# Attention and two feed-forward layers on one core: weights decoded in pairs of chunks, through two raw buffers of 1 MB

## The chip, the core and the metric

One core of a Trainium2 chip runs the whole program. The metric is the device time of one execution in microseconds. A kernel's time is the median over its runs, and one further execution is taken with the hardware profiler; all rows shown come from that one.

## The reference

Inputs are float32. Attention has no softmax over scores: q is normalised by exp over its feature axis, k by exp over the sequence, and the product is q (k^T v). Two feed-forward layers follow on all 2304 tokens.

```python
q_s = exp(q - max(q, -1)); q_s /= sum(q_s, -1) + 1e-9      # (4, 8, 576, 64)
k_s = exp(k - max(k, 2));  k_s /= sum(k_s, 2) + 1e-9
x = q_s @ (k_s^T @ v)                                      # to (2304, 512)
h = x @ w_in1;  x = (h * sigmoid(1.702 h)) @ w_out1        # w_in (512, 2048)
h = x @ w_in2;  out = (h * tanh(softplus(h))) @ w_out2     # w_out (2048, 512)
```

The four weight matrices reach the kernel as float64, so it must decode them on the chip. It makes two float32r parts of each weight, a high one and the rest, and forms each product from three matmuls (high x high, high x rest, rest x high; `SPLIT`).

## The kernel before

Tokens are cut into 6 blocks of 384 (`NB`), the feed-forward width into 16 chunks of 128 (`NFC`). For each block, `attention(blk)` makes the block's x in the buffer `xt[blk % 2]`. The first layer then runs over block and chunk: `gemm_in1(n)` (L755, 12 matmuls of 384 columns), `gelu` and `gelu_split` (L768, L773 and the lines of `copy` and `either`), and `gemm_out` (L796, 12 matmuls) two chunks later. All these GEMMs write the key `spine`, so they keep their order on TensorE. `x2_evac` stores the layer's result. The second layer does the same by pairs of chunks (`gemm_in2`, `mish`, `gemm_out2` at L927) and `out_evac` copies the result through the tiles `dec` to the output.

**Weights.** `weight(m, io, fc)` (L366) decodes one chunk of w_in (`io` 0) or w_out (`io` 1), 512 weights per partition. A DMA on SP's queue (L320) brings 512 KB into one of four buffers `raw`; each weight is two 32-bit words, `lo_w` and `hi_w`, which lie alternately. Then come:

- two scalings, normally on ScalarE (L346): `hi_w` into one of three tiles `dec`, `lo_w` in place in `raw`;
- on VectorE the fast shift (L386), the OR with the sign (L393, reads `hi_w`) and the addition of the low word (L398, the last reader of `raw`);
- the copy of the high part into the weight tile `W` (L337, ScalarE or VectorE) and the subtraction that gives the rest (L329, VectorE or GpSimd). This frees `dec`.

Each chunk has one tile `W[fc]` for both its matrices. The first 13 are there from the start; the last three (`NLATE`) use memory that `attention(0)` sets free. The second layer's chunks are decoded into the same tiles as soon as the first layer's last block has read them. `w_order(lag)` gives the order: w_in runs ahead of w_out by 2 chunks in the first layer and 6 in the second.

**Order of the work.** Nothing is issued as the loops reach it. Each operation goes into a `Plan` with its ways (an engine and a cost for each), the keys that it reads and those that it writes. `Plan.order` then plays all engines and the one DMA queue forward by these costs (`act_ns`, `dve_ns`, `pool_ns`, `mm_ns`; a DMA of n bytes counts n / 280 ns and 650 at least), takes the most urgent operation that is ready, and picks the engine where it ends first. `best` does so six times, with urgencies from a pass backwards, and keeps the shortest. `emit` issues the result in that order, so each engine and SP's queue works through a fixed list, and an instruction that waits holds those behind it on its own list. Before the first GEMM the plan also places idle transposes on TensorE (L962).

The buffers are keys like all others; this is what makes a load wait for the addition of the chunk that had its buffer before:

```python
r, a = raw[i % NRAW], dec[i % ND]
rl, rh, da = ("raw", i % NRAW, 0), ("raw", i % NRAW, 1), ("dec", i % ND)
...
dma(P * 4096, [], [rl, rh], lambda: dst, lambda: src)
```

Of the kernel before, what the change touches and what calls it, by code (L numbers as in the profile page):

```python
# [19 lines left out]
class Plan:  # L20
# [13 lines left out]
    def __init__(self):  # L34
        self.ops = []
        self.first = None
        self.last_write = {}
        self.readers = {}
# [37 lines left out]
    def order(self, links, urgency, ways=None):  # L76
# [125 lines left out]
def pool_ns(n):  # L202
    return {512: 1256.0, 384: 972.0, 768: 1800.0}[n]
# [7 lines left out]
def tile_attention_moe_moe(  # L211
# [35 lines left out]
    NLATE = 3  # L247
    NRAW = 4
    WHOLE = 2
    ND = 3  # L250
# [8 lines left out]
    W = [const.tile([P, 2, 1024], F32R, name=f"W{i}") for i in range(NFC - NLATE)]  # L259
# [3 lines left out]
    raw = [const.tile([P, 1024], I32, name=f"raw{i}") for i in range(NRAW)]  # L263
    dec = [const.tile([P, 512], I32, name=f"dec{i}") for i in range(ND)]
# [78 lines left out]
    def scaled(out, in_, scale, reads, writes):  # L343
        plan.op(
            [
                (ACT, act_ns(512), lambda: nc.scalar.activation(out=out, in_=in_, func=AF.Copy, scale=scale), False),  # L346
                (
                    DVE,
                    dve_ns(512, True),
                    lambda: nc.vector.tensor_single_scalar(out=out, in_=in_, scalar=scale, op=ALU.mult),  # L350
                    True,
                ),
            ],
            reads,
            writes,
        )
# [9 lines left out]
    def weight(m, io, fc):  # L366
# [22 lines left out]
        dve(  # L389
            512,  # L390
            [rh],
            [da],
            lambda: nc.vector.scalar_tensor_tensor(  # L393
                out=a, in0=hi_w, scalar=-0x80000000, in1=a, op0=ALU.bitwise_and, op1=ALU.bitwise_or
            ),
            pair=True,
        )
        dve(512, [rl], [da], lambda: nc.vector.tensor_tensor(out=a, in0=a, in1=lo_w, op=ALU.add), pair=True)  # L398
        late = [("late",)] if fc >= NFC - NLATE else []
        copy(512, lambda: W[fc][:, io, 0:512], lambda: f32(a), [da] + late, [("W", io, fc, 0)])  # L400
        either(
            512,
            ALU.subtract,
            lambda: W[fc][:, io, 512:1024],
            lambda: f32(a),
            lambda: f32(W[fc][:, io, 0:512]),
            [da, ("W", io, fc, 0)],
            [("W", io, fc, 1)],
        )

    def w_mm(fc, io, part, c, n=P):
        return W[fc][:, io, part * 512 + c * P : part * 512 + c * P + n]

# [336 lines left out]
    def gemm_in(h, hkeys, buf, fc, ccs=range(NCC)):  # L750
        for cc in ccs:
# [11 lines left out]
            pe(3 * mm_ns(NB), x_keys(buf, cc) + [("W", 0, fc, 0), ("W", 0, fc, 1)], [spine] + hkeys, mm)  # L763
# [26 lines left out]
    def gemm_out(n):  # L790
        fc = n % NFC
        for dm in range(NCC):

            def mm(dm=dm):
# [11 lines left out]
                [("W", 1, fc, 0), ("W", 1, fc, 1), ("g", n % 2, 0), ("g", n % 2, 1)],  # L806
# [32 lines left out]
    ob = [f32(t) for t in dec]  # L839
# [5 lines left out]
    def pool_first():  # L845
        sctx.close()
        late = ctx.enter_context(tc.tile_pool(name="late", bufs=1, side="right", reuse_waits="tile"))
        W.extend(late.tile([P, 2, 1024], F32R, name=f"W{i}") for i in range(NFC - NLATE, NFC))
# [69 lines left out]
    def gemm_out2(n):  # L918
        bi, pr = divmod(n, NPR)
        gi = (n + 1) % NGP  # L920
        for j in range(2):
            for c in range(NCT):
# [12 lines left out]
                wk = [("W", 1, 2 * pr + j, a) for a in range(2)]  # L935
                pe(3 * mm_ns(512), wk + [("gg", gi, 0), ("gg", gi, 1)], [spine, ("acc", bank)], mm)

    def out_evac(bi):
        blk = blocks[bi]
        dst = out[blk * NB : (blk + 1) * NB, :].rearrange("(p c) e -> p c e", c=NCT)  # L940
        for c in range(NCT):
# [8 lines left out]
                [("dec", c)],  # L950
            )
            dma(P * 2048, [("dec", c)], [], lambda c=c: dst[:, c, :], lambda o=o: o)


    def w_order(lag):
        seq = [(0, fc) for fc in range(lag)]
        for fc in range(lag, NFC):
            seq += [(0, fc), (1, fc - lag)]
        return seq + [(1, fc) for fc in range(NFC - lag, NFC)]
# [5 lines left out]
    FIRST_W = 24  # L965
# [10 lines left out]
    for io, fc in w_order(2):  # L976
        weight(0, io, fc)
    second = w_order(6)
# [43 lines left out]
    for n in range(NSB + LAG):  # L1022
        if n < NSB:
            weights_to(FIRST_W + 4 * n)
# [43 lines left out]
```

## Time and profile before

| | before |
|---|---|
| median of 3 runs | 892.43 us |
| lowest, highest | 891.02, 893.08 us |
| profiled execution | 891.93 us, its span 890.2 us |
| busy: PE, DVE, ACT, POOL | 99%, 44%, 41%, 1% of the span |
| raw loads, 512 KB each | 32 of w_in, 32 of w_out; 4.3 and 4.0 us to landing (median) |
| HBM read, written | 54.00 MB, 11.01 MB |

PE stands for TensorE's matmuls, PEld for its weight loads, DVE for VectorE, ACT for ScalarE, POOL for GpSimd, SP for the queue from which all DMAs are issued. The span runs from the first to the last instruction of the program; the execution's own time has a little around it. Busy shares of the whole span mix stages with different limits, so tables by stretch and the chain of waits are read beside them. In the chain, each piece is what the next one waited for, or the instruction before it on the same engine, and its time is what it adds to the chain. The granted clock of TensorE is shown as 1.00 throughout.

### The profile page before, as it was taken

Reading aid. Unit: us, or ns where it says so; the run is one execution under the profiler, and the core shown is the slowest. Engines: PE = TensorE matmul, PEld = TensorE weight load, DVE = VectorE, ACT = ScalarE, POOL = GpSimd, SP = SyncE. Lnnn points to the kernel's source line nnn. Section 1 sums busy time; section 2 is a strip of 40 time slices with the busy share of each in tenths; the row PEclk is TensorE's granted clock in tenths of the full one; section 3 lists DMA queues with packets and bytes.
Section 4 is the critical chain, followed back from the end, with each engine's and each line's share of the span. In section 5 each row is a group of like instructions: output and inputs, shape, how many; then the busy total and the mean of one; then the engine's idle time right before and its main releaser. Section 6 shows DMA issues by size and latency. Waiting matters only on the chain.

```text
span 890.2 us, 12245 instructions
## 1 busy us (share of the span) xinstructions
PE 880.3 (99%) x4961; PEld 818.9 (92%) x4961; DVE 394.6 (44%) x757; ACT 362.7 (41%) x649; POOL 5.3 (1%) x21
## 2 busy tenths in 40 slices
PE   8999999999999999999999999999999999999998
PEld 5897899999999999999999999899899899899896
DVE  7999993263385276226999911101101101111110
ACT  6987863242343244224778821321321321321321
POOL 1000000000000000000000000000000000000000
PEclk9999999999999999999999999999999999999999
DMA  9676762011132022100355301001001001000000
GB/s 259 201 221 175 202 209 70 5 48 55 27 94 95 1 71 55 48 1 18 119 168 187 119 1 71 36 1 71 36 1 71 36 1 71 36 1 0 36 1 36
DMA packets 62712, 65.80 MB, mean 74 GB/s; under 512 B 32448, under 2 KB 53696, under 8 KB 62144
## 3 DMA queue, kind: packets, MB, share of 16 engines
q1 hardware_dynamic: 62656, 65.02, 23.7%
q8 instruction: 39, 0.64, 0.3%
q14 instruction: 17, 0.14, 0.0%
HBM read 54.00 MB, written 11.01 MB: 73 GB/s over the span
## 4 chain that ended last, share of the span: by engine, by line
PE 88%; DVE 7%; ACT 2%; DMA 1%; issue 1%; DVEq 0%; SPq 0%
PE hp L755 23%; PE acc L927 22%; PE acc L796 19%; PE h L755 19%; DVE dec L393 1%; DVE dec L398 1%; PE at L533 1%; DVE W L329 1%; DMA raw<-in_moe_w_in_dram 1%; PE at L667 1%; PE at L638 1%; PE acc L494 1%; DVE gt L773 1%; PE acc L497 1%; DVE dec L386 1%
## 5 line engine op out<-in xcount | busy, mean ns | idle before, releaser
L755 PE MATMUL h<-xt,W 128*128 128x384 f32 x1152 | 224.3, 339 | 1.0 <-DVE gt L773 0.8
L796 PE MATMUL acc<-g,W 128*128 128x384 f32 x1152 | 223.0, 339 | 0.2 <-DVE W L329 0.2
L755 PE MATMUL hp<-xt,W 128*128 128x384 f32 x1152 | 208.4, 335 | 0.0
L927 PE MATMUL acc<-W,g 128*128 128x512 f32 x864 | 206.1, 392 | 0.0
L755 PEld LDWEIGHTS hp<-xt,W 128*128 128x128 f32 x1152 | 201.9, 188 | 3.7
L755 PEld LDWEIGHTS h<-xt,W 128*128 128x128 f32 x1152 | 200.4, 188 | 5.2 <-DVE gt L773 1.1
L796 PEld LDWEIGHTS acc<-g,W 128*128 128x128 f32 x1152 | 200.5, 188 | 2.7 <-issue 0.8
L927 PEld LDWEIGHTS acc<-W,g 128*128 128x128 f32 x864 | 161.6, 188 | 32.7
L329 DVE TENSOR_TENSOR g<-gt,g 128x384 fp32r<-128x384 f32 (+1 forms) x110 | 67.4, 613 | 179.0 <-ACT g L337 178.7
L329 DVE TENSOR_TENSOR g<-tb,g 128x768 fp32r<-128x768 f32 x32 | 30.7, 958 | 211.6 <-ACT g L337 211.6
L904 ACT ACTIVATE tb<-hp 128x768 f32<-128x768 f32 x32 | 26.0, 812 | 177.7 <-PE hp L755 177.7
L337 ACT ACTIVATE g<-gt 128x384 fp32r<-128x384 f32 (+1 forms) x112 | 63.8, 570 | 80.0 <-PE acc L796 77.4
L768 ACT ACTIVATE gt<-h 128x384 f32<-128x384 f32 x96 | 46.9, 488 | 92.7 <-PE h L755 92.6
L773 DVE SCALAR_TENSOR_TENSOR gt<-gt,h 128x384 f32<-128x384 f32 x96 | 52.8, 550 | 63.8 <-ACT gt L768 63.5
L904 ACT ACTIVATE gt<-hp 128x768 f32<-128x768 f32 x16 | 13.0, 814 | 96.3 <-PE hp L755 96.3
L346 ACT ACTIVATE dec<-raw 128x512 f32<-128x512 f32 x64 | 42.9, 675 | 10.1 <-DVE W L329 8.9
L346 ACT ACTIVATE raw<-raw 128x512 int32<-128x512 uint32 x63 | 42.0, 676 | 4.8 <-DMA raw<-in_moe_w_out_dram 3.0
L329 DVE TENSOR_TENSOR W<-dec,W 128x512 fp32r<-128x512 f32 x64 | 43.6, 683 | 0.8 <-ACT W L337 0.5
L398 DVE CUSTOM_DVE_ANT_0 dec<-raw,dec 128x1024 uint16<-128x1024 uint16 x64 | 43.6, 683 | 0.4
L393 DVE SCALAR_TENSOR_TENSOR dec<-raw,dec 128x512 int32<-128x512 int32 x64 | 43.6, 683 | 0.2
L337 ACT ACTIVATE W<-dec 128x512 fp32r<-128x512 f32 x62 | 38.9, 630 | 7.3 <-DVE dec L398 7.3
L337 ACT ACTIVATE g<-tb 128x768 fp32r<-128x768 f32 x32 | 27.1, 847 | 1.0
(78 smaller groups left out, 396.8 us busy)
## 6 DMA issues: line engine op xcount, KB each, us to landing
raw<-in_moe_w_in_dram SPq DMA_DIRECT2D x32, 512.0 KB, 4.3
raw<-in_moe_w_out_dram SPq DMA_DIRECT2D x32, 512.0 KB, 4.0
x2d<-xt SPq DMA_DIRECT2D x16, 384.0 KB, 3.1
xt<-x2d SPq DMA_DIRECT2D x4, 1536.0 KB, 6.5
kt<-in_k_dram SPq DMA_DIRECT2D x16, 288.0 KB, 4.3
out_dram<-dec SPq DMA_DIRECT2D x18, 256.0 KB, 2.1
vt<-in_v_dram SPq DMA_DIRECT2D x24, 144.0 KB, 3.5
qt<-in_q_dram SPq DMA_DIRECT2D x24, 96.0 KB, 2.6
```

Source lines behind the costliest of these rows:

```text
L329: return lambda: engine.tensor_tensor(out=out(), in0=in0(), in1=in1(), op=op)
L337: (ACT, act_ns(n), lambda: nc.scalar.activation(out=out(), in_=in_(), func=AF.Copy), False),
L346: (ACT, act_ns(512), lambda: nc.scalar.activation(out=out, in_=in_, func=AF.Copy, scale=scale), False),
L386: lambda: nc.vector.tensor_single_scalar(out=a, in_=a, scalar=3, op=ALU.logical_shift_left),
L393: lambda: nc.vector.scalar_tensor_tensor(out=a, in0=hi_w, scalar=-0x80000000, in1=a, op0=ALU.bitwise_and, op1=ALU.bitwise_or),
L398: dve(512, [rl], [da], lambda: nc.vector.tensor_tensor(out=a, in0=a, in1=lo_w, op=ALU.add), pair=True)
L755: nc.tensor.matmul(out=h(), lhsT=w_mm(fc, 0, a, cc), rhs=xt[buf][:, cc, b, :], start=cc == 0 and i == 0, stop=cc == NCC - 1 and i == 2,)
L768: act(NB, [hk, ("tables",)], [tk], lambda: nc.scalar.activation(out=t, in_=h, func=AF.Tanh, scale=0.851), psum=True)
L773: lambda: nc.vector.scalar_tensor_tensor(out=t, in0=t, scalar=1.0, in1=h, op0=ALU.add, op1=ALU.mult),
L796: nc.tensor.matmul(out=acc[dm][:, 0:NB], lhsT=w_mm(fc, 1, a, dm), rhs=g[n % 2][:, b, :], start=fc == 0 and i == 0, stop=fc == NFC - 1 and ...
L904: nc.scalar.activation(out=tb[i], in_=hb(n), func=AF.Mish)
L927: nc.tensor.matmul(out=acc[bank], lhsT=g2[gi][:, j, a, c * P : (c + 1) * P], rhs=w_mm(2 * pr + j, 1, b, 0, 512), start=pr == 0 and j == 0 ...
```

## The change

Two neighbouring chunks are decoded together. `weight(m, io, fp)` works on pair `fp` (8 of them, `NFP`): one DMA of 1 MB into one of two buffers `raw` of twice the size, and operations of 1024 elements through two tiles `dec` of twice the size. The DMA of w_in now reads 512 32-bit words of a row where it read 256. `W` becomes a tile per pair and matrix, `W[fp][io]`, with the two chunks side by side; the last two pairs (four chunks) are those that wait for `attention(0)`'s memory. `either` and the scalings are costed for 1024 elements, and POOL has a cost for that length. Waits of matmuls on weights go by pairs (`fc // 2`, `pr`). The lags become 1 and 3 pairs, `FIRST_W` 12 pairs, and `weights_to` grows by 2 pairs per step. A new table `soonest` keeps the first two raw loads from being planned before 12 us. The output goes through halves of the two `dec` tiles, under keys `ob` of its own.

```diff
-    return {512: 1256.0, 384: 972.0, 768: 1800.0}[n]
+    return {1024: 2400.0, 512: 1256.0, 384: 972.0, 768: 1800.0}[n]
...
-                t = 0.0
+                t = 0.0 if ways else self.soonest.get(i, 0.0)
...
-    NLATE = 3
-    NRAW = 4
+    NLATE = 2
+    NRAW = 2
     WHOLE = 2
-    ND = 3
+    ND = 2
+    NFP = NFC // 2
+    FIRST_LOAD = 12000.0
...
-    W = [const.tile([P, 2, 1024], F32R, name=f"W{i}") for i in range(NFC - NLATE)]
+    W = [[const.tile([P, 2, 1024], F32R, name=f"W{i}_{io}") for io in range(2)] for i in range(NFP - NLATE)]
...
-    raw = [const.tile([P, 1024], I32, name=f"raw{i}") for i in range(NRAW)]
-    dec = [const.tile([P, 512], I32, name=f"dec{i}") for i in range(ND)]
+    raw = [const.tile([P, 2048], I32, name=f"raw{i}") for i in range(NRAW)]
+    dec = [const.tile([P, 1024], I32, name=f"dec{i}") for i in range(ND)]
...
         if io == 0:
             dst = r.rearrange("p (cc f) -> p cc f", cc=NCC)
-            src = w_ap[m][0][:, fc * 256 : (fc + 1) * 256].rearrange("(cc p) f -> p cc f", p=P)
+            src = w_ap[m][0][:, fp * 512 : (fp + 1) * 512].rearrange("(cc p) f -> p cc f", p=P)
+            at_w = lambda part: W[fp][0][:, :, part * 512 : (part + 1) * 512].rearrange("p l (cc f) -> p l cc f", cc=NCC)
+            of = f32(a).rearrange("p (cc l f) -> p l cc f", cc=NCC, l=2)
         else:
-            dst = r
-            src = w_ap[m][1][fc * P : (fc + 1) * P, :]
-        dma(P * 4096, [], [rl, rh], lambda: dst, lambda: src)
+            dst = r.rearrange("p (l e) -> p l e", l=2)
+            src = w_ap[m][1][fp * 256 : (fp + 1) * 256, :].rearrange("(l p) e -> p l e", p=P)
+            at_w = lambda part: W[fp][1][:, :, part * 512 : (part + 1) * 512]
+            of = f32(a).rearrange("p (l e) -> p l e", l=2)
+        if i < NRAW:
+            plan.soonest[len(plan.ops)] = FIRST_LOAD
+        dma(P * 8192, [], [rl, rh], lambda: dst, lambda: src)
         scaled(f32(a), f32(hi_w), 2.0**-112, [rh], [da])
         scaled(lo_w, lo_w.bitcast(U32), 2.0**-29, [], [rl])
         dve(
-            512,
+            1024,
...
-        copy(512, lambda: W[fc][:, io, 0:512], lambda: f32(a), [da] + late, [("W", io, fc, 0)])
+        copy(1024, lambda: at_w(0), lambda: of, [da] + late, [("W", io, fp, 0)])
...
-    ob = [f32(t) for t in dec]
+    ob = [f32(dec[c // 2])[:, c % 2 * 512 : (c % 2 + 1) * 512] for c in range(NCT)]
...
-                [("dec", c)],
-            )
-            dma(P * 2048, [("dec", c)], [], lambda c=c: dst[:, c, :], lambda o=o: o)
+                [("ob", c)] + ([("dec", i) for i in range(ND)] if bi == 0 else []),
+            )
+            dma(P * 2048, [("ob", c)], [], lambda c=c: dst[:, c, :], lambda o=o: o)
...
-    FIRST_W = 24
+    FIRST_W = 12
...
-    for io, fc in w_order(2):
-        weight(0, io, fc)
-    second = w_order(6)
+    for io, fp in w_order(1):
+        weight(0, io, fp)
+    second = w_order(3)
...
-            weights_to(FIRST_W + 4 * n)
+            weights_to(FIRST_W + 2 * n)
```

## Rows read from the trace of the kernel before

**Rows 1.** The head of the page: busy us (share of the span) and instructions.

```profile
PE 880.3 (99%) x4961; PEld 818.9 (92%) x4961; DVE 394.6 (44%) x757; ACT 362.7 (41%) x649; POOL 5.3 (1%) x21
```

**Rows 2.** Table by stretches: busy us of PE, PEld, DVE, ACT, POOL; clock; DMA.

```profile
60.00:119.30 59.30, 57.09 (x356) 47.44 (x354) 58.74 (x127) 48.33 (x100) 2.37 (x2) 1.00 0.68 196
119.30:416.00 296.70, 296.70 (x1851) 292.02 (x1852) 148.77 (x305) 109.08 (x220) 0.00 (x0) 1.00 0.18 53
416.00:510.00 94.00, 94.00 (x533) 92.86 (x532) 88.47 (x165) 71.98 (x133) 0.00 (x0) 1.00 0.44 140
```

**Rows 3.** The chain of waits, 34 to 125 us: start us, us, piece.

```profile
37.12 0.47 DVE g L329
37.59 0.60 DVE dec L393
...
40.32 0.60 DVE W L329
...
59.25 4.79 DMA raw<-in_moe_w_in_dram
...
70.94 0.87 DVE qt L329
...
72.42 0.34 DVE dec L386
...
118.61 0.31 ACT kv L556
...
119.89 2.08 PE h L755 x12
```

**Rows 4.** The page's groups: out<-in, shape, count; busy us, mean ns; idle before.

```profile
L329 DVE TENSOR_TENSOR g<-tb,g 128x768 fp32r<-128x768 f32 x32 | 30.7, 958 | 211.6 <-ACT g L337 211.6
...
L346 ACT ACTIVATE dec<-raw 128x512 f32<-128x512 f32 x64 | 42.9, 675 | 10.1 <-DVE W L329 8.9
...
L329 DVE TENSOR_TENSOR W<-dec,W 128x512 fp32r<-128x512 f32 x64 | 43.6, 683 | 0.8 <-ACT W L337 0.5
```

**Rows 5.** DMA issues from 0 to 13 us: count, KB each, median us to landing.

```profile
raw<-in_moe_w_out_dram SPq DMA_DIRECT2D x1, 512.0 KB, 10.8
```

**Rows 6.** Timeline, 9 to 18 us: start us, us, instruction.

```profile
9.53 1.71 SPq L320 DMA_DIRECT2D raw<-in_moe_w_out_dram  x1
...
14.40 0.68 ACT L346 ACTIVATE dec<-raw 128x512 f32<-128x512 f32 x1
```

**Rows 7.** Timeline at the end of the decode, 116 to 128 us.

```profile
118.45 0.68 DVE L398 CUSTOM_DVE_ANT_0 dec<-raw,dec 128x1024 uint16<-128x1024 uint16 x1
...
121.03 0.68 DVE L329 TENSOR_TENSOR W<-dec,W 128x512 fp32r<-128x512 f32 x1
...
121.81 2.25 PE L796 MATMUL acc<-g,W 128*128 128x384 f32 x12
```

**Rows 8.** Waits of SP's queue: us in total, times, longest.

```profile
SPq L320 <- DVE dec L398: 143.2, 51, 19.1
```

**Rows 9.** Operations on raw, 43 to 62 us: loads issued, first and last start, landing.

```profile
L320 SPq DMA_DIRECT2D raw<-in_moe_w_in_dram x4: 373/373/373, 43.9 to 59.3; - x4
...
DMA to landing us min/median/max: 3.8/4.3/4.8
```

**Rows 10.** The same from 39 to 41 us.

```profile
L320 SPq DMA_DIRECT2D raw<-in_moe_w_in_dram x1: 378/378/378, 39.3 to 39.3; - x1
L320 SPq DMA_DIRECT2D raw<-in_moe_w_out_dram x1: 340/340/340, 40.4 to 40.4; - x1
...
DMA to landing us min/median/max: 3.6/4.4/5.3
```

**Rows 11.** The same over the span: ns min/median/max, first and last start.

```profile
L398 DVE CUSTOM_DVE_ANT_0 dec<-raw,dec x64: 674/682/694, 16.9 to 509.6; 128x1024 uint16<-128x1024 uint16 x64
```

**Rows 12.** Waits of DVE from 10 to 119 us: us in total, times, longest.

```profile
DVE W L329 <- ACT W L337: 0.5, 1, 0.5
```

**Rows 13.** The chain of waits, 480 to 560 us.

```profile
536.95 4.17 PE hp L755 x24
```

More of the change, by code (lines that the diff above doesn't have):

```diff
@@ L36, in __init__ @@
         self.first = None
+        self.soonest = {}
         self.last_write = {}
@@ L345, in scaled @@
             [
-                (ACT, act_ns(512), lambda: nc.scalar.activation(out=out, in_=in_, func=AF.Copy, scale=scale), False),
+                (ACT, act_ns(1024), lambda: nc.scalar.activation(out=out, in_=in_, func=AF.Copy, scale=scale), False),
                 (
                     DVE,
-                    dve_ns(512, True),
+                    dve_ns(1024, True),
                     lambda: nc.vector.tensor_single_scalar(out=out, in_=in_, scalar=scale, op=ALU.mult),
@@ L364, in tile_attention_moe_moe, with weight @@
     n_w = [0]
-    def weight(m, io, fc):
+    def weight(m, io, fp):
         i = n_w[0]
@@ L389, in weight @@
         dve(
-            512,
+            1024,
             [rh],
@@ L397, in weight @@
         )
-        dve(512, [rl], [da], lambda: nc.vector.tensor_tensor(out=a, in0=a, in1=lo_w, op=ALU.add), pair=True)
-        late = [("late",)] if fc >= NFC - NLATE else []
-        copy(512, lambda: W[fc][:, io, 0:512], lambda: f32(a), [da] + late, [("W", io, fc, 0)])
+        dve(1024, [rl], [da], lambda: nc.vector.tensor_tensor(out=a, in0=a, in1=lo_w, op=ALU.add), pair=True)
+        late = [("late",)] if fp >= NFP - NLATE else []
+        copy(1024, lambda: at_w(0), lambda: of, [da] + late, [("W", io, fp, 0)])
         either(
-            512,
+            1024,
             ALU.subtract,
[L404 to L408, printed above, removed]
+            lambda: at_w(1),
+            lambda: of,
+            lambda: f32(at_w(0)),
+            [da, ("W", io, fp, 0)],
+            [("W", io, fp, 1)],
         )
     def w_mm(fc, io, part, c, n=P):
-        return W[fc][:, io, part * 512 + c * P : part * 512 + c * P + n]
+        return W[fc // 2][io][:, fc % 2, part * 512 + c * P : part * 512 + c * P + n]
     qT = [g2[1][:, i] for i in range(2)]
@@ L761, in mm @@
                     )
-            pe(3 * mm_ns(NB), x_keys(buf, cc) + [("W", 0, fc, 0), ("W", 0, fc, 1)], [spine] + hkeys, mm)
+            pe(3 * mm_ns(NB), x_keys(buf, cc) + [("W", 0, fc // 2, 0), ("W", 0, fc // 2, 1)], [spine] + hkeys, mm)
     def gelu(n):
@@ L805, in gemm_out @@
                 3 * mm_ns(NB),
-                [("W", 1, fc, 0), ("W", 1, fc, 1), ("g", n % 2, 0), ("g", n % 2, 1)],
+                [("W", 1, fc // 2, 0), ("W", 1, fc // 2, 1), ("g", n % 2, 0), ("g", n % 2, 1)],
                 [spine, ("acc", dm)],
@@ L847, in pool_first @@
         late = ctx.enter_context(tc.tile_pool(name="late", bufs=1, side="right", reuse_waits="tile"))
-        W.extend(late.tile([P, 2, 1024], F32R, name=f"W{i}") for i in range(NFC - NLATE, NFC))
+        W.extend([late.tile([P, 2, 1024], F32R, name=f"W{i}_{io}") for io in range(2)] for i in range(NFP - NLATE, NFP))
     def pool_second():
@@ L933, in mm @@
                         )
-                wk = [("W", 1, 2 * pr + j, a) for a in range(2)]
+                wk = [("W", 1, pr, a) for a in range(2)]
                 pe(3 * mm_ns(512), wk + [("gg", gi, 0), ("gg", gi, 1)], [spine, ("acc", bank)], mm)
@@ L949, in out_evac @@
                 [("acc", (bi * NCT + c) % 4)],
-                [("dec", c)],
+                [("ob", c)] + ([("dec", i) for i in range(ND)] if bi == 0 else []),
             )
-            dma(P * 2048, [("dec", c)], [], lambda c=c: dst[:, c, :], lambda o=o: o)
+            dma(P * 2048, [("ob", c)], [], lambda c=c: dst[:, c, :], lambda o=o: o)
     def w_order(lag):
[L956 to L959, printed above, removed]
+        seq = [(0, fp) for fp in range(lag)]
+        for fp in range(lag, NFP):
+            seq += [(0, fp), (1, fp - lag)]
+        return seq + [(1, fp) for fp in range(NFP - lag, NFP)]
     def idle():
```

## The prediction, made before the kernel was run

> **What bounds the kernel now.** I read the page's head first: PE is counted as busy for 99% of the span [rows 1]. Spans of matmuls overlap, so I went on to the table by stretches, where PEld (weight loads) tells whether matmuls really follow one another. From 119.3 to 510 us PE has no gap (PEld 292.02 of 296.70 us and 92.86 of 94.00) [rows 2]. From 60 to 119.3 us PEld is at 47.44 of 59.30 us only, while DVE is busy 58.74 of 59.30 us and ACT 48.33. So one stretch has a limit other than PE: there the first layer's weights are decoded beside attention(1) and the first GEMMs, and DVE is that limit. The chain of waits says the same: from 37.12 us on it goes along DVE nearly from one instruction to the next, turns to ACT and PE at 118.61 us for the last product of attention(1), and from 119.89 us it is PE alone, in steps of 2.08 us [rows 3]. What shortens DVE's list of work ahead of 119.3 us shortens the kernel one for one; after that point only a new gap on PE counts.
>
> **The DVE work that the change removes.** In the chain, a 512-element OR (L393) or subtraction (W L329) hands on after 0.60 us and the fast shift (L386) after 0.34 us [rows 3]; these steps are shorter than the 683 ns that one lasts by the page's groups [rows 4], since the end of one lies beside the start of the next. The step grows with the length: 0.47 us for 384 elements (g L329), 0.87 for 768 (qt L329) [rows 3], so 0.40 us for 384 more, 1.04 ns an element, which leaves 0.07 us that doesn't depend on the length. An operation of 1024 then takes 0.07 + 1.07 = 1.14 us where two took 1.20. The shift runs at twice the rate; no longer one is in the trace, and I give it the same 0.07. Each pair of chunks drops four DVE operations (shift, OR, addition, subtraction), 4 x 0.07 = 0.28 us. A layer has 32 chunks (64 subtractions in two layers [rows 4]), 16 pairs: **4.4 us off DVE**. The bounds: nothing, if the step of 1024 is twice that of 512; at most 8.5 us, if each dependent operation shows its whole duration, since the groups have 683 ns for 512 and 958 for 768 [rows 4], hence some 1.23 us for 1024 against 1.37 for two, 0.13 x 64. I take 4.4, as DVE is packed and so goes by steps.
>
> **What it removes on ACT** (two scalings and a copy per chunk, 16 x 3 operations less) counts for nothing: ACT has 11 us free from 60 to 119.3 us, and DVE none [rows 2]. DVE covers it; were ACT the later one, a gain of about the same size would come from there instead.
>
> **First loads.** Before, four raw loads of 512 KB went out among attention's loads into a full queue; the last was issued at 9.5 us and landed after 10.8, at 20.3 us [rows 5, 6], and the first chunk's scaling began at 14.40 us [rows 6]. Now the two loads of 1 MB may not be planned before 12 us, which puts them behind attention's loads. The bytes are the same, so I expect the second by 20.3 us too and the first between 16 and 18. At worst DVE starts its first decode 18 - 14.4 = 3.6 us later with nothing else to do; at best attention(0), whose loads have the queue to themselves, fills that time and comes earlier by a microsecond. It has most of its DVE work ready then, so I take +0.5 us.
>
> **End of the stretch.** W_out 14 and 15 now become ready together. Before, gemm_out(14) began at 121.81 us and chunk 15's last subtraction ended at 121.03 + 0.68 = 121.71 [rows 7], needed only at gemm_out(15), two GEMMs later. Now both chunks must be done by gemm_out(14). With everything 4.4 us earlier the pair ends at 117.3 and is wanted at 117.4: it fits, with nothing to spare. Taken: +0.2 us; bounds 0 and 4.2 (two GEMMs of 2.1).
>
> **The ring of buffers.** A load of raw waits on SP for the addition that frees its buffer, 143.2 us in 51 waits [rows 8], so every load goes out the moment its buffer is free, and what stands behind it on SP (k, v and q of attention(1)) is held with it. Before, in the tightest stretch, four w_in loads, every second one of the queue, were issued from 43.9 to 59.3 us and landed after 4.3 (the median there) [rows 9]: a buffer came round once in 2 x 15.4 / 3 = 10.3 us, of which it lay filled or in decoding for a stay r = 6.0. Now there are two buffers of twice the size. For 1 MB I take the two loads issued one behind the other at 39.3 and 40.4 us, the longest landing 5.3 us after its issue [rows 10]: D = 6.4 us. A filled buffer needs at least a scaling, the shift, the OR and the addition: 0.68, 0.34, 0.68 and 0.68 us for 512 elements [rows 3, 4, 11], 2.4 in all; with 512 more elements at DVE's 1.04 ns each, the shift at half of that and ACT's scaling taken alike, r is about 4.2 us at best. Eight fills of each buffer give a last release at 20.3 + 7(D + r) + r: with r = 4.2 that is 98.7 us, with r = 6.0 113.1. The last addition ended at 118.45 + 0.68 = 119.1 before [rows 7], and a gain of 4.4 needs 114.7. So the ring just keeps up, as other DVE work (gelu, attention(1)) can fill its gaps. Some will stay: operations of 1.1 us stand longer in DVE's order, and a subtraction waits for a longer copy on ACT (one wait of 0.5 us before [rows 12]). Taken: +0.5 us; bounds 0 and the slower rival below. The Trainium skill, page SBUF — State Buffer, section The DMA setup-cost knee, fits a transfer as 2 us plus its bytes at 436 GB/s. For 512 KB that is 3.2 us, and the trace's median in this stretch is 4.3 [rows 9], so the measurement decides; by its 4.4 us for 1 MB the ring would be further from a limit, and the sum the same.
>
> **After 119.3 us** nothing is priced. The second layer's decode lies under a full PE: its last addition starts at 509.6 us [rows 11], while the last pair of w_in is first used at 536.95 us [rows 13] and w_out later still. That decode can end 27 us later before PE sees it. Output copies only get other addresses in dec.
>
> **Sum.** -4.4 + 0.5 + 0.2 + 0.5 = -3.2 us. Against the profiled execution (891.93 us, its span 890.2 and 1.7 us around it) that is 888.7; the median of the three runs, 892.43, is 0.5 above it, so I predict **889.2 us**. A measurement of this kernel can tell about 0.2%, 1.8 us, from no change: faster means below 890.6, slower above 894.2.
>
> **Rivals.**
> 1. *The gaps eat it* (same). DVE loses 0.28 us of work per pair and gets it back as waits: 0.2 us more per pair, for the copy on ACT or for a scaling, is 16 x 0.2 = 3.2 us instead of my 0.5, and leaves -0.5 us, 891.9. For: only two pairs are in work at a time. Against: with 58.74 of 59.30 us busy [rows 2] DVE always had other work at hand.
> 2. *The two buffers become the bound* (slower). Above r = 6.75 us the formula's last release lies behind the 119.1 us of before. A chunk needed 2.4 of its stay of 6.0, so it queued for 3.6; if a pair queues as long on top of its 4.2, r = 7.8, the last release is at 20.3 + 7 x 14.2 + 7.8 = 127.5 us, 8.4 late, and the time 900.8. Half-way, at r = 7.2, it is 122.7, 3.6 late and 896.0. For: a raw load was on the chain already (4.79 us at 59.25) [rows 3]. Against: with two pairs in flight instead of four chunks there is less to queue behind. The Trainium skill speaks for this rival: Perfetto Trace Analysis, section DMA Optimizations, says that splitting transfers into smaller chunks may let some of them start sooner; this change goes the other way. No row of the kernel before can show which is the stronger here.
> 3. *The end doesn't move* (same): attention(1) and not the decode ends the stretch, as its last pieces at 118.61 us run over ACT and PE [rows 3], and the planner leaves them at the old time: 892.4. Against: the chain was led there by DVE all the way.
>
> **Chances.** The forecast 0.58, rival 1 0.15 and rival 3 0.05, rival 2 0.22, with most of that up to 4 us late. The range leaves some 5% below 886.8 (towards the bound of 8.5 us) and 15% above 896.5 (half-way in rival 2 and beyond); the forecast's own is 886.8 to 890.6.
>
> **What would show it.** Right: PE's unbroken stretch starts 2 to 4 us before 119.3; L393 and L398 last about 1.22 us, 16 of each ahead of it; DVE stays busy to 98% from 60 us on; raw loads land in about 6 us. Rival 2: DVE or ACT waits for raw again and again, near 1 us each. Wrong altogether: a gap on PE behind 120 us, or decode operations of 1024 that last longer than two of 512.

## The result and the profile after

The changed kernel takes 899.25 us (median of 4 runs, 898.14 to 899.4) where the kernel before takes 892.42 (891.02 to 893.08). The ratio is 1.0071, 95% interval 1.0059 to 1.0084, that is 5.3 to 7.5 us; between the medians it is 6.8 us slower, where 3.2 us faster was forecast, and above the upper end of the range, 896.5. The profiled execution has a span of 897.4 us, 7.2 more than before. One execution of run 8's kernel, 1240.15 us at a granted clock of 0.655, was in a slower state of the chip and is left out of that run's median below.

First the head of the page of the changed kernel, busy time and instructions by engine:

```profile
PE 882.6 (98%) x4973; PEld 822.0 (92%) x4973; DVE 395.8 (44%) x647; ACT 336.9 (38%) x536; POOL 4.6 (1%) x20
```

Against [rows 1] DVE has 110 instructions fewer and ACT 113. The 32 pairs of both layers should drop 4 each on DVE, 128, and 3 each on ACT, 96. So some 17 operations have moved from ACT to DVE, and DVE's busy time has not shrunk (394.6 us before). The table of the same three stretches says where the time went; its first edge is moved to 126.70 us, where the chain of waits shows the first product of the second token block (before: 119.89 us [rows 3]):

```profile
60.00:126.70 66.70, 63.08 (x395) 56.39 (x394) 66.50 (x105) 45.46 (x72) 1.66 (x1) 0.97 0.69 205
126.70:416.00 289.30, 289.30 (x1807) 284.57 (x1807) 138.89 (x284) 102.68 (x207) 0.00 (x0) 1.00 0.18 53
416.00:510.00 94.00, 93.78 (x537) 92.78 (x536) 83.45 (x114) 59.78 (x85) 0.00 (x0) 1.00 0.37 124
```

From 126.7 us on it is [rows 2] again: PE without a gap, the second layer's decode under it. The unbroken stretch begins 6.8 us later, and that is the whole loss. Ahead of it DVE is busy for 66.50 of 66.70 us, even fuller than before. So the question is what happens in the first 126 us.

The best measure of progress there is how many matmuls of the first layer's products have been done at a given time (h of gemm_in and acc of gemm_out, 12 matmuls each). The groups of PE from 0 to 80 us in the kernel before:

```profile
L755 PE MATMUL h<-xt,W 128*128 128x384 f32 x132 | 26.3, 344 | 1.0 <-DVE gt L773 0.8
L796 PE MATMUL acc<-g,W 128*128 128x384 f32 x102 | 20.4, 344 | 0.2 <-DVE W L329 0.2
```

and in the changed kernel:

```profile
L766 PE MATMUL h<-xt,W 128*128 128x384 f32 x108 | 22.3, 350 | 2.8 <-DVE gt L784 1.9 <-DVE xt L641 1.0
L807 PE MATMUL acc<-g,W 128*128 128x384 f32 x82 | 17.4, 360 | 1.1 <-DVE W L333 1.1
```

234 matmuls against 190 by 80 us. Twelve take 2.08 us [rows 3], so 44 missing ones are 7.6 us, about the loss. At 60 us it is 165 against 119, 46 missing: the products fell behind before 60 us, and nothing was regained after. The chain of waits of the changed kernel shows why not (start us, us, piece):

```profile
37.48 1.14 DVE dec L404
39.14 2.98 PE h L766 x12
...
60.69 1.13 DVE dec L409
62.43 0.65 DVE dec L397
...
73.03 1.14 ACT dec L350
...
77.51 3.34 PE acc L807 x12
80.86 2.52 PE h L766 x12
83.37 2.08 PE acc L807 x12
...
126.70 2.11 PE h L766 x12
```

Before, the chain went along DVE nearly all the way to 118.61 us [rows 3]. Now it lies on PE from 39.14 to 56.3 us, goes back to DVE and ACT, and from 77.21 us on is PE alone: there PE has a backlog of products as long as the rest of the stretch. A faster DVE is worth nothing once PE is behind. The decode itself did not end later than before: the last addition of the first layer starts at 117.8 us, and the last subtraction ends at 120.51 + 1.22 = 121.73 us, where it was 118.45 and 121.71 before [rows 7]. The additions of the decode from 12 to 126 us (count, ns min/median/max, first and last start), and that last subtraction:

```profile
L409 DVE CUSTOM_DVE_ANT_0 dec<-raw,dec x16: 1197/1217/1226, 23.2 to 117.8; 128x2048 uint16<-128x2048 uint16 x16
120.51 1.22 DVE L333 TENSOR_TENSOR W<-dec,W 128x1024 fp32r<-128x1024 f32 x1
```

So the last weights came as early as before, 7 us ahead of gemm_out(14) at 128.81 us, and the loss lies in products that came too late long before them. The 2.98, 3.34 and 2.52 us for twelve matmuls are taken up in the last section.

Two more views answer to the prediction's. DVE's decode groups from 0 to 126.7 us:

```profile
L404 DVE SCALAR_TENSOR_TENSOR dec<-raw,dec 128x1024 int32<-128x1024 int32 x17 | 20.7, 1216 | 0.0
L409 DVE CUSTOM_DVE_ANT_0 dec<-raw,dec 128x2048 uint16<-128x2048 uint16 x16 | 19.5, 1216 | 0.1
L333 DVE TENSOR_TENSOR W<-dec,W 128x1024 fp32r<-128x1024 f32 x16 | 19.4, 1216 | 0.0
L397 DVE TENSOR_SCALAR dec<-dec 128x1024 int32<-128x1024 int32 x17 | 11.7, 686 | 1.0 <-ACT dec L350 1.0
...
L354 DVE TENSOR_SCALAR raw<-raw 128x1024 int32<-128x1024 uint32 x5 | 3.4, 687 | 0.0
...
L354 DVE TENSOR_SCALAR dec<-raw 128x1024 f32<-128x1024 f32 x2 | 1.4, 683 | 0.0
...
L340 DVE CAST W<-dec 128x1024 fp32r<-128x1024 f32 x1 | 0.7, 693 | 0.0
```

The long operations cost what was priced: 1216 ns long, and the chain steps mostly by 1.14 and 1.13 us, where two of 512 took 1.20. But the last three lines are new work on DVE. Scalings (L354) and a copy to W (L340) may go to either engine, and the planner gives them to the one that ends first. In the same stretch the kernel before had a single one of them on DVE:

```profile
L350 DVE TENSOR_SCALAR raw<-raw 128x512 int32<-128x512 uint32 x1 | 0.4, 421 | 0.0
```

The chain steps by 0.61 us over such a scaling (at 31.87 and 61.82 us), so eight are 4.9 us where the one of before took some 0.3: about as much as the 4.4 us that the longer operations had freed.

The raw loads, count, KB, median us to landing, from the page's DMA issues:

```profile
raw<-in_moe_w_in_dram SPq DMA_DIRECT2D x16, 1024.0 KB, 5.7
raw<-in_moe_w_out_dram SPq DMA_DIRECT2D x16, 1024.0 KB, 4.9
```

The prediction's ring took 6.4 us for 1 MB, so the loads landed sooner than it had them.

### The profile page after: what moved, and what is told of

Same layout as the page of the kernel before. It is cut to its first block, busy times and chain, and to the rows that moved or that the text cites. A ratio compares the mean times of both kernels' runs of the same rounds, so it can differ in the third digit from the quotient of the medians.

```text
span 897.4 us, 11975 instructions
## 1 busy us (share of the span) xinstructions
PE 882.6 (98%) x4973; PEld 822.0 (92%) x4973; DVE 395.8 (44%) x647; ACT 336.9 (38%) x536; POOL 4.6 (1%) x20
## 4 chain that ended last, share of the span: by engine, by line
PE 92%; DVE 4%; DMA 1%; ACT 1%; issue 1%; SPq 0%; DVEq 0%; ACTq 0%
PE hp L766 22%; PE acc L938 22%; PE acc L807 21%; PE h L766 21%; PE at L544 2%; DMA kt<-in_k_dram 1%; DVE dec L404 1%; PE at L678 1%; PE at L649 1%; PE at L687 1%; PE at L505 1%; PE at L508 1%; DVE dec L409 1%; DVE dec L397 0%; DVE W L333 0%
## 5 line engine op out<-in xcount | busy, mean ns | idle before, releaser
L333 DVE TENSOR_TENSOR W<-dec,W 128x1024 fp32r<-128x1024 f32 x32 | 39.0, 1217 | 2.2 <-ACT W L341 2.2
L409 DVE CUSTOM_DVE_ANT_0 dec<-raw,dec 128x2048 uint16<-128x2048 uint16 x32 | 39.0, 1218 | 0.4
L404 DVE SCALAR_TENSOR_TENSOR dec<-raw,dec 128x1024 int32<-128x1024 int32 x32 | 39.0, 1218 | 0.3
L350 ACT ACTIVATE dec<-raw 128x1024 f32<-128x1024 f32 x29 | 33.3, 1149 | 3.9 <-DMA raw<-in_moe_w_in_dram 2.9
L341 ACT ACTIVATE W<-dec 128x1024 fp32r<-128x1024 f32 x27 | 28.7, 1062 | 15.1 <-DVE dec L409 15.1
L350 ACT ACTIVATE raw<-raw 128x1024 int32<-128x1024 uint32 x24 | 27.8, 1156 | 0.0
```

Of the source, the lines that this page charges most:

```text
L333: return lambda: engine.tensor_tensor(out=out(), in0=in0(), in1=in1(), op=op)
L341: (ACT, act_ns(n), lambda: nc.scalar.activation(out=out(), in_=in_(), func=AF.Copy), False),
L350: (ACT, act_ns(1024), lambda: nc.scalar.activation(out=out, in_=in_, func=AF.Copy, scale=scale), False),
L404: lambda: nc.vector.scalar_tensor_tensor(out=a, in0=hi_w, scalar=-0x80000000, in1=a, op0=ALU.bitwise_and, op1=ALU.bitwise_or),
L409: dve(1024, [rl], [da], lambda: nc.vector.tensor_tensor(out=a, in0=a, in1=lo_w, op=ALU.add), pair=True)
```

## The experiments

Three suspects were left by the traces: **P**, both chunks of a pair become usable only together, so PE gets its weights late and in lumps; **the ring**, two buffers that are filled and emptied as a whole; **the planner's choice**, ScalarE work moved onto the full DVE. A fourth, small one is the first loads, held back to 12 us. Each was put into the kernel before, or taken out of the changed kernel. The kernel before was measured again beside the runs, at 892.38 us (runs 1 to 4), 892.66 (5 to 8) and 892.80 (9 and 10), and the ratios are against these; the changed kernel was not, so differences from it are against the 899.25 us of its four runs. Every edit also makes the planner work out the whole order anew, so a part of each difference can be the new order and not the cause that the edit aims at. In the expectations P, R, S and F stand for the late pairs, the ring, the planner's choice and the first loads.

**1. Only the second layer in pairs** (`layer2_only`), the first one chunk by chunk as before:

```diff
+    MERGE1 = lambda io, fp: False
+    MERGE2 = lambda io, fp: True
...
     def weight(m, io, fp):
+        if (MERGE2 if m else MERGE1)(io, fp):
+            unit(m, io, fp, [0, 1])
+        else:
+            unit(m, io, fp, [0])
+            unit(m, io, fp, [1])
```

> Pairs in the second layer alone; the first layer decodes chunk by chunk through the same memory (four quarters of the two raw tiles), with no delay of the first loads. All theories put the loss ahead of the point where TensorE becomes gapless, so all expect the time of the kernel before: 892.4 +- 1.5 us. If the second layer's decode had a share in it, 894 or more, with a gap on TensorE behind 400 us.

Measured 893.31 us, ratio 1.0017 [1.0002, 1.0031], span 890.2, that of the kernel before to the tenth. Of the 0.9 us between the medians most comes from three of its ten executions, of 895.9 to 896.5 us, which the last section takes up; the other seven have a median of 892.66. The second layer has no share that counts, and loads and operations of twice the length do no harm under a full PE. The loss is in the first layer.

**2. Pair readiness and the order by pairs** (`pair_ready`): the kernel before with its 512-element operations, its four buffers and loads, but the subtractions of a pair come last, the odd chunk's first, and the even chunk's waits for it. Order and lags go by pairs as in the change.

```diff
+    def weight(m, io, fp):
+        got = [start(m, io, 2 * fp + j) for j in range(2)]
+        for j in (1, 0):
+            fc = 2 * fp + j
+            a, da = got[j]
+            either(
+                512,
...
+                [da, ("W", io, fc, 0)] + ([] if j else [("W", io, fc + 1, 1)]),
+                [("W", io, fc, 1)],
+            )
```

> The kernel before, with four buffers of 512 KB and operations of 512, but both chunks of a pair become usable together: the even chunk's last subtraction stands behind the odd one's, and the order goes by pairs. Theory P (a pair comes too late as a whole; TensorE starves early and has no time left at the end): 4 to 8 us slower than before, 896 to 900, with TensorE starved between 60 and 80 us. Theory R (two raw buffers hold the loads back): no change, 891 to 894. Theory S (ScalarE's work moved to VectorE) and theory F (first loads late): no change.

Measured 900.44 us, ratio 1.0086 [1.0060, 1.0112]: as much as the whole loss within the noise, 8.0 us, with no operation longer and no buffer fewer. PE's groups from 0 to 80 us in this kernel:

```profile
L762 PE MATMUL h<-xt,W 128*128 128x384 f32 x108 | 22.8, 353 | 0.8 <-DVE gt L780 0.6 <-DVE xt L637 0.2
L803 PE MATMUL acc<-g,W 128*128 128x384 f32 x82 | 16.1, 340 | 2.0 <-DVE W L329 1.7 <-DVE g L329 0.3
```

190 matmuls by 80 us, the same number as the changed kernel, and most of the idle time ahead of acc is put down to the subtraction into W, as P says. The table of ten-microsecond stretches has PE down to 7.99 and 7.35 us busy:

```profile
60.00:70.00 10.00, 7.99 (x57) 6.63 (x56) 10.00 (x20) 8.00 (x16) 1.04 (x1) 1.00 0.57 189
70.00:80.00 10.00, 7.35 (x43) 6.65 (x42) 8.51 (x19) 7.23 (x15) 2.36 (x1) 1.00 0.80 201
```

DVE has gaps here too (8.51 of 10), and from 60 to 97 us the chain of waits passes twice over a load of raw (5.78 us at 67.86, 5.55 us at 88.43). The weights also come in the order of the pairs, and the even chunk holds its dec tile until the odd one is done. So a part of the 8.0 us may come from this order and from loads that it delays, and not from PE's waits alone; the run cannot part these.

**3. The loads alone** (`pair_loads`): two buffers of 1 MB, both halves sent when the whole buffer is free, the first not before 12 us, but operations of 512 elements on three dec tiles, and each chunk usable by itself. The weights come in the order of the pairs here too, and of the two halves the odd chunk's is sent first, so that the even chunk, which is wanted first, lands last.

```diff
+        if i < NRAW:
+            plan.soonest[len(plan.ops)] = FIRST_LOAD
+        plan.op([(DMA, P * 8192 / 280.0, loads, False)], [], keys)
+        late = [("late",)] if fp >= NFP - NLATE else []
+        for l in range(2):
+            chunk(m, io, fp, l, r, i % NRAW, late)
```

> The changed kernel's loads alone: two buffers of 1 MB, both halves sent for when the whole buffer is free, the first not before 12 us; but operations of 512 elements on three dec tiles, and each chunk usable for itself. Theory R: nearly the whole loss, 897 to 901. Theory P: little of it, 892 to 895. Theory F: 2 to 4 us, 894 to 896, with the first scaling at 19 us and the first GEMM at 29 us or later.

Measured 896.98 us, ratio 1.0058 [1.0036, 1.0081]: 4.6 us slower than before, at the lower edge of what R expected and above what P did. So the loads cost something without longer operations or joint readiness, and far more than the 0.5 + 0.5 us that I gave them; the order by pairs is in the 4.6 us. By 80 us 216 matmuls are done.

**4. Scalings and copies on ScalarE only** (`act_only`), otherwise the changed kernel:

```diff
-                (
-                    DVE,
-                    dve_ns(1024, True),
-                    lambda: nc.vector.tensor_single_scalar(out=out, in_=in_, scalar=scale, op=ALU.mult),
-                    True,
-                ),
...
-        copy(1024, lambda: at_w(0), lambda: of, [da] + late, [("W", io, fp, 0)])
+        act(1024, [da] + late, [("W", io, fp, 0)], lambda: nc.scalar.activation(out=at_w(0), in_=of, func=AF.Copy))
```

> The changed kernel, but the scalings and the copies to W may run on ScalarE alone (in the changed kernel VectorE took 16 of 96 from it). Theory S: about 16 x 0.6 us = up to 5 us less work on VectorE ahead of the point where TensorE becomes gapless, so 2 to 5 us faster than the changed kernel, 894 to 897. Theories P, R and F: within 1.5 us of the changed kernel, 898 to 901.

Measured 897.01 us, ratio 1.0059 [1.0042, 1.0075], 2.2 us less than the changed kernel. The two intervals overlap, so the size is uncertain; the span says 2.6 (894.8 against 897.4) and the matmuls done by 80 us are 211 against 190.

**5. The kernel before with late first loads** (`late_loads`):

```diff
+        if i < NRAW:
+            plan.soonest[len(plan.ops)] = 12000.0
```

> The kernel before with one part of the change, its first raw loads (four of 512 KB) not planned before 12 us. Theory F: a good part of the loss, 895 or more. Theories P, R and S: at most 1 us, 892 to 893.5.

Measured 893.97 us, ratio 1.0018 [1.0006, 1.0030]: 1.3 us between the medians, between the two expectations.

**6. Half the bytes** (`half_bytes`): the changed kernel, whose loads after the first two bring only half of each pair; the other half is decoded from what the buffer still holds.

```diff
-        dma(P * 8192, [], [rl, rh], lambda: dst, lambda: src)
+        if i < NRAW:
+            dma(P * 8192, [], [rl, rh], lambda: dst, lambda: src)
+        elif io == 0:
+            dma(P * 4096, [], [rl, rh], lambda: dst[:, 0:2], lambda: src[:, 0:2])
+        else:
+            dma(P * 4096, [], [rl, rh], lambda: dst[:, 0], lambda: src[:, 0])
```

> The changed kernel, but after the first two loads each load of raw brings only half of its bytes (512 KB; the other half of the buffer keeps older weights, so half of the weights are not the layer's). A load then lands in about 4.3 us in place of 5 to 6. Theory R: shorter loads ease the ring, 2 to 4 us faster than the changed kernel, 895 to 897. Theories P and S: within 1 us of it, 898 to 900.

Measured 896.24 us, ratio 1.0046 [1.0030, 1.0061], 3.0 us less than the changed kernel. Loads to landing from 12 to 126 us, min/median/max, in the changed kernel and then in this one:

```profile
DMA to landing us min/median/max: 4.7/5.6/10.8
```

```profile
DMA to landing us min/median/max: 3.1/3.4/4.6
```

A load lands 2.2 us sooner by the median. The buffers come round only a little sooner: the first layer's later loads into one buffer follow each other after 11.6 and 11.8 us on average (one figure for each buffer), where it was 12.1 and 12.6 in the changed kernel. So the size of the loads costs some 3 us in the changed kernel, as R expected; whether through the buffers, or through the queue that attention(1)'s loads share with them, this run does not part. The Trainium skill, page Perfetto Trace Analysis, section DMA Optimizations, says that splitting may let some transfers start sooner. No run here shows it: run 6 halves the bytes as well, and run 3, which sends two loads of 512 KB for a pair, sends both only when the whole buffer is free.

**7. Even chunks not held back** (`even_early`): the changed kernel, in which an even chunk of the first block's products reads the previous chunk's weights, and so never waits for its own pair.

```diff
+    def ready(n):
+        fc = n % NFC
+        return fc - 1 if n < NFC and fc > 0 and fc % 2 == 0 else fc
...
-                [("W", 1, fc // 2, 0), ("W", 1, fc // 2, 1), ("g", n % 2, 0), ("g", n % 2, 1)],
+                [("W", 1, rc // 2, 0), ("W", 1, rc // 2, 1), ("g", n % 2, 0), ("g", n % 2, 1)],
```

> The changed kernel, but in the first block of the first layer the GEMMs of an even chunk (2, 4, ...) read the weights of the chunk before it, so an even chunk waits for the pair before its own and only the odd chunk for its own pair; the product of the even chunks is left out. Theory P: the wait for whole pairs is most of the loss, 3 to 6 us faster than the changed kernel, 893 to 896, with the granted clock at 1.00 again after 45 us. Theories R and S: within 1.5 us of it, 898 to 900.

Measured 896.02 us, ratio 1.0040 [1.0027, 1.0054], 3.2 us less than the changed kernel, 226 matmuls by 80 us. The clock did not do as expected: it is 0.83 from 80 to 90 us. P counts within the full change too, but for less than the 8.0 of run 2. That the same microseconds are also claimed by the ring and by DVE's load, so that taking one claim away leaves the others, would explain it; run 8 speaks against much of such overlap.

**8. All three taken out** (`all_three`): the edits of 4, 6 and 7 together.

> The changed kernel with three edits together: even chunks early (as in even_early, their products left out), scalings and copies to W on ScalarE alone, and loads of half the bytes after the first two (half of the weights not the layer's). If P, R and S are the whole of what went wrong, the 4.4 us that the longer operations take off VectorE come out: 2 to 4 us faster than the kernel before, 888 to 890.5. If something else costs in the longer operations themselves, 893 or more.

Measured 890.86 us, ratio 0.9980 [0.9971, 0.9990]: 8.4 us less than the changed kernel, where the three alone sum to 2.2 + 3.0 + 3.2 = 8.4, and 1.8 us less than the kernel before. It lies between the two expectations. PE's groups to 80 us:

```profile
L765 PE MATMUL h<-xt,W 128*128 128x384 f32 x132 | 26.7, 347 | 0.1
L811 PE MATMUL acc<-g,W 128*128 128x384 f32 x103 | 19.8, 337 | 0.0
```

235 matmuls, one more than before, and hardly an idle moment ahead of them. The table of this kernel from 40 to 120 us (PE busy first, then PEld, DVE, ACT, POOL, clock):

```profile
40.00:60.00 20.00, 20.00 (x116) 19.89 (x115) 20.00 (x26) 15.38 (x22) 0.00 (x0) 1.00 0.27 88
60.00:80.00 20.00, 20.00 (x131) 19.02 (x129) 19.94 (x28) 16.07 (x22) 0.00 (x0) 1.00 0.46 135
80.00:100.00 20.00, 19.99 (x118) 16.56 (x117) 19.44 (x34) 16.65 (x27) 2.77 (x1) 1.00 0.43 129
100.00:120.00 20.00, 19.97 (x141) 17.54 (x140) 19.32 (x36) 15.72 (x27) 0.00 (x0) 1.00 0.49 134
```

PE is busy for 79.96 of 80 us: once the three are out, PE and not DVE is the limit from 40 us on, and DVE's shorter list can give no more. How much of the 1.8 us is DVE's shorter list can't be read from this run, since edits 6 and 7 also take away waits that the kernel before has itself.

**9. TensorE kept awake** (`warm_gaps`): the changed kernel with idle transposes also between the first block's products.

```diff
-        nc.tensor.transpose(hps[1][:, 0:P], ident, ident)
+        for i in range(2):
+            if filling.count(i) % 12 == 0:
+                nc.tensor.transpose(hps[i][:, NB : NB + P], ident, ident)
+                return
```

> The changed kernel, in which TensorE transposes an identity matrix into an unused half of an h tile whenever it would stand idle, now also between the products of the first block (as before only ahead of the first product); nothing of the result changes. Theory C (the granted clock): in the changed kernel twelve matmuls took 2.98 us at 39 us and 3.34 us at 77 us where 2.08 is usual, each after TensorE had been idle part of the time, and the clock of those ten microseconds was 0.83 and 0.91. If this is a loss of its own, worth the 2.0 and 1.7 us that these records show, the kernel is 1.7 to 3.7 us faster than the changed one: 895.5 to 897.5, and no twelve matmuls of h or acc take over 2.3 us between 40 and 120 us. Rival W (the late weights): the slow products lie in time that TensorE would have waited for weights anyway; then the time stays within 1.5 us of 899.25 although the clock no longer falls.

Measured 904.32 us, ratio 1.0132 [1.0115, 1.0150]: 5.1 us slower than the changed kernel, which neither side expected. The granted clock did stay at 1.00 in every stretch of the first 140 us, and twelve matmuls of a product took 2.08 to 2.29 us in the chain. But the filling got in the way. Its own line among PE's groups, 30 to 130 us:

```profile
L978 PE MATMUL h<-ident 128*128 128x128 f32 x87 | 11.5, 276 | 4.9 <-ACT gt L780 4.2 <-DVE gt L785 0.7
```

PE stood 4.9 us ahead of transposes that waited for gelu to finish reading the h tile, and the products stood behind them. The order is a new one here too: DVE is busy for 8.86 us from 60 to 70 us, where the changed kernel has 10.00. So the waits of the filling are a likely cause of the 5.1 us, but not shown to be all of it. By 80 us only 180 matmuls were done. So the run is no test of what the lower clock costs.

**10. Edit 4 with first loads from 4 us on** (`act_early`):

```diff
-    FIRST_LOAD = 12000.0
+    FIRST_LOAD = 4000.0
```

> The changed kernel with scalings and copies on ScalarE alone (as act_only, 897.0) and the first two loads of weights allowed from 4 us on in place of 12. Theory F: the late first loads cost 1.3 us when put into the kernel before by themselves; if that is a part of the loss that adds to the rest, the time is 1 to 1.6 us below that of act_only: 895.4 to 896.0. Rival: attention(0) loses to the 2 MB on the queues what the decode gains (its loads are then behind or beside the weights), and the time is 897 or above.

Measured 895.53 us, ratio 1.0032 [1.0021, 1.0044]: 1.5 us below run 4, near the 1.3 us that run 5 gave to the first loads. The granted clock differs with them, 0.996 to 0.998 over the executions of run 4 and 0.999 to 1.000 here, so the 1.5 us need not be the earlier loads by themselves. It is the fastest form of the change itself, 3.7 us below it, and still 2.7 us above its runs of the kernel before (892.80). A third buffer of 1 MB wasn't tried.

All runs, by the matmuls of h and acc counted in the groups to 60 and to 80 us:

| kernel | to 60 us | to 80 us | median us |
|---|---|---|---|
| before | 165 | 234 | 892.4 |
| all_three | 139 | 235 | 890.9 |
| layer2_only | 162 | 231 | 893.3 |
| even_early | 134 | 226 | 896.0 |
| late_loads | 138 | 221 | 894.0 |
| act_early | 112 | 216 | 895.5 |
| half_bytes | 130 | 216 | 896.2 |
| pair_loads | 138 | 216 | 897.0 |
| act_only | 116 | 211 | 897.0 |
| changed | 119 | 190 | 899.3 |
| pair_ready | 128 | 190 | 900.4 |
| warm_gaps | 120 | 180 | 904.3 |

The column at 80 us puts the kernels nearly in the order of their times; the one at 60 doesn't. A gap before 60 us can be made up while PE still has idle time ahead of it; from 80 us on PE is busy nearly throughout in the kernel before as well, and there is little left to use.

## Why the prediction was wrong

**What bounds the kernel: "one for one" was wrong.** "What shortens DVE's list of work ahead of 119.3 us shortens the kernel one for one" holds while DVE is the last to finish and PE has idle time to give up. I took PE's idle time from PEld, which leaves 11.9 us free from 60 to 119.3 us [rows 2]. But PEld isn't full even where PE is the limit. In the changed kernel the chain lies on PE alone from 77.21 us, and the table has (PE busy first, then PEld):

```profile
80.00:100.00 20.00, 20.00 (x121) 18.39 (x121) 20.00 (x29) 12.71 (x18) 0.67 (x1) 0.96 0.62 197
100.00:120.00 20.00, 19.97 (x121) 16.63 (x120) 19.83 (x35) 16.67 (x29) 0.99 (x1) 1.00 0.75 205
```

Here PEld is 35.02 of 40 us with PE busy for 39.97. By PE's own busy time only 2.2 us were free before (57.09 of 59.30) [rows 2], less than the 4.4 us that were to come out. I never asked how late the early products could become before PE, and not DVE, sets the end. In the changed kernel this happened at 77 us.

**DVE's 4.4 us: right in size, lost in the plan.** The step of 1024 is 1.13 to 1.14 us, as worked out, and the shift's at its shortest 0.60 against 0.61. But "counts for nothing" for ACT was the wrong question. I asked whether ACT would be late, and it wasn't; the planner still put eight of its operations on DVE, 4.9 us, where it had put one. A likely reason, not tested: in the planner's costs (`act_ns`, `dve_ns`) a scaling of 1024 takes 948 ns on ACT and 602 on DVE, where one of 512 took 521 and 336, so that DVE's lead has grown from 185 to 346 ns and it is more often the one that ends first. Run 4 gives 2.2 us for undoing it. The signs that I named for being right all came but the first: operations of 1.22 us, DVE at 99% from 60 us on, loads landing in about 6 us. They show that the costs were right, and say nothing of what comes out at the end.

**End of the stretch, +0.2 with bounds 0 and 4.2: the step that failed worst.** I priced the joint readiness at the last pair of w_out alone. There it cost nothing: the pair was ready at 121.73 us and wanted at 128.81. It holds for every pair: each even chunk, of w_in and w_out, waits for its neighbour's decode, and the first ones are wanted when PE has no other products to do. Run 2 has 8.0 us for this together with the order by pairs, run 7 has 3.2 us within the full change. Run 8 keeps the order by pairs and loses nothing, so that order alone is not a large cost.

**The ring, +0.5: mis-sized.** The formula compared the last release with 119.1 us and found it in time, and it was: the last addition ended at 117.83 + 1.22 = 119.05 us. But the loads cost by when the early weights come, not by when the last buffer is free. Run 6 has 3.0 us, run 3 4.6 us with the first loads and the order by pairs in it. The 6.4 us that the formula took for a load of 1 MB was long: the medians are 5.7 and 4.9 us. A buffer came round in 12.1 and 12.6 us on average, at the slow end of the formula's 10.6 to 12.4. SP waited 59.2 us in 13 waits for the addition up to 126 us, where it was 51.7 us in 23 up to 119 us before. The sign that I named for Rival 2, waits of ACT and DVE for raw of near 1 us each, hardly came: ACT waited twice, 2.9 us in all. So it isn't Rival 2 as I told it. That the measured 899.25 us lies within its 896 to 900.8 is luck: its mechanism, a late last release, was not what was seen.

**First loads, +0.5: 1.3 to 1.5** by runs 5 and 10, with the clock in both figures (last section): the six executions of run 5 with a clock of 0.998 or more have a median of 893.16 us, 0.5 above the kernel before.

**After 119.3 us, nothing: right.** Run 1 has the second layer in pairs and the span of before; behind 126.7 us PE is as full as it was.

**The sum, put right:** in the changed kernel 3.2 (pairs) + 3.0 (size of the loads) + 2.2 (planner) + 1.5 (first loads) = 9.9 us of losses by the runs that undo each, over a net loss of 6.8. Run 8 bears out the first three together, with 8.4 us; how they part it is less certain, since every run has its own order. The rest, 3.1 us, would be the gain from longer operations, below the 4.4 that I had; it is a difference of large numbers whose intervals overlap, and run 8's caution holds for it too. A figure worked out, not one measured; in run 8, with PE full from 40 us on, 1.8 us came out.

The Trainium skill, page Perfetto Trace Analysis, section Optimizing Scalar/DVE Operations, has both sides of this case: it says that larger operations can help an engine that is saturated, and that breaking instructions up may help where an engine that isn't saturated leaves bubbles on others. Here DVE was saturated and left bubbles on PE as well. For the first the runs have 0.06 us per merged pair of operations (1.14 against 1.20); for the second no run breaks operations up, and run 2 only shows what it costs when two chunks become ready together.

## What to carry to other kernels

When work is merged into larger units, price the wait of every consumer that now needs the whole unit, above all the first ones, and not only the cost of the operations or the last unit. Ask of each stretch how much idle time the engine behind the bottleneck has: here some 2 us by PE's own busy time, and once PE was behind, at 77 us, a faster producer was worth nothing. Where a planner chooses between engines, an edit of sizes changes its choices, so count each engine's instructions anew.

## What the runs showed of the hardware

TensorE's granted clock fell in the starved part of the changed kernel, where before it was 1.00 from 60 us on [rows 2]. The table of ten-microsecond stretches of the changed kernel (PE busy first, then PEld, DVE, ACT, POOL, clock):

```profile
30.00:40.00 10.00, 7.18 (x36) 5.71 (x35) 10.00 (x19) 7.84 (x14) 0.00 (x0) 1.00 0.72 196
40.00:50.00 10.00, 10.00 (x46) 8.37 (x45) 9.59 (x13) 6.52 (x10) 0.00 (x0) 0.83 0.49 157
...
70.00:80.00 10.00, 7.49 (x38) 6.72 (x37) 10.00 (x15) 6.05 (x12) 0.00 (x0) 0.91 0.68 201
80.00:90.00 10.00, 10.00 (x52) 9.35 (x52) 10.00 (x15) 6.40 (x9) 0.00 (x0) 0.92 0.66 220
```

Means of 0.83, 0.91 and 0.92 are mixtures of the two levels, 2.4 and 1.2 GHz. Each fall follows a stretch in which PE was idle for a quarter of the time, and the products right after it are those that took longest in the chain: 2.98, 3.34 and 2.52 us for twelve matmuls where 2.08 is usual, 2.6 us more in all. Two pieces of attention(1) behind the first of them, 1.51 and 0.93 us where 0.65 is usual, add 1.1. So here a starved PE was also a slower one. But it need not be: in run 2 PE is busy for only 7.35 us from 70 to 80 us, in run 6 for 7.57, and the clock stays at 1.00 in this stretch and the next.

What the lower clock costs is not settled. All these longer pieces, 3.7 us in excess, lie on the chain of waits, and the four runs of the changed kernel all have a mean clock of 0.996 or 0.997; so it can be up to half of the loss, as a part of how late products cost and not beside it. Two other kernels show that a lower clock can go with a longer time: the four executions of run 5 with a mean clock of 0.996 have a median of 895.32 us against 893.16 for the other six, and the three of run 1 with 0.995 to 0.997 have 895.88 against 892.66. The mean clock is no price by itself: one execution of the kernel before has 0.949 at 892.82 us, and run 8's go from 890.03 to 892.93 us at 0.996 to 0.998. The kernel of run 2 lost 8 us, with a profile at a clock of 1.00 from 30 to 90 us, so a loss of this size does not need the lower clock; and run 9 held the clock at 1.00 with idle transposes and was slower.

A scaling of 1024 elements lasts 0.69 us on DVE, against 1.15 on ACT, and its step is 0.61 us: DVE is the faster engine for it. That a planner which asks only who ends first sends it for this reason to the engine that has no time fits the costs, but no run tested it.
